# A ninth gate/up pair made inside the recurrence, and the values of segments 54 to 57 made in the opening

## The chip, the core and the metric

One core of a Trainium2 chip. The time is the device time of one execution in microseconds; the kernel before was timed three times, and its median counts. A second figure is used beside it: the span of one profiled execution, whose trace gives every row that is quoted.

## What is computed

A pre-norm block over 2048 rows of 640 columns: `h = x + A(layernorm(x))`, then `h2 = h + B(layernorm(h))`.

```
for s in range(64):                              # A: 64 segments of 32 rows
    h = concat([mem, xs])                        # 8 memory rows + 32 rows of x
    q, k, v = h Wq, h Wk, h Wv                   # 32 heads of 128
    p = softmax(where(mask, q k^T * scale, -1e9))
    o = (p v) Wo
    mem = o[:8]; outs.append(o[8:])              # the next segment's memory
# B: h = relu(x Wgate) * (x Wup), 1728 columns; out = h Wdown
```

The memory rows make A a chain: segment s+1 needs the first eight output rows of segment s. B has no such chain.

## The kernel before

Every instruction is added to a list, in program order, by hand; a solver (L46) turns the tiles that each reads and writes into semaphore waits, and each engine then runs its own instructions strictly in that order. So the place of an `add` or `dma` in the program is its place in its engine's queue. `dma` (L353) uses SP's queue where nothing else is said. A PSUM bank is a tile of its own (`B(n)`): a product that writes it waits for the copy that read it last. The banks are BQ (0, 1), T0, T1 (2, 3) and P0 to P3 (4 to 7).

**The opening** (L765 to L1134) loads the weights: Wk, Wq, Wv (`W`, 15 loads) and Wo (8 loads, L787). It makes segment 0 as soon as its weights are there, and some projections for later segments. `far_part` (L853) makes keys and queries of the late rows of segments 54 to 57 from `a3`, rows of x that depend on no memory. `far_tok` (L861) copies the banks P0 and P1 to `tok` on ScalarE, `far_flip` (L864) transposes them on VectorE, `far_save` (L868) keeps them in DRAM (`next_d[2]`, `next_d[3]`). Other held rows are saved at L1127 by `held_saves`. While the second half of Wo lands in quarters, the loop at L1120 puts one quarter of `wo_pass`, one chunk of a value projection (`xe`) and `keep_busy(2)` (L1072, matmuls whose result nobody reads) behind each other. Then come the load of the next 128 rows into `xl` (`ln1_load`, L1129), `to_act_split` (L1130, the memory rows for step 1), the copies of the banks BQ to `Ve[0]` (L1132) and the moments of `xl` (`row_moments`, L1134, on VectorE).

**The steps** (L1145 to L1339): one per segment, 1 to 63. Each projects keys (to P2, P3), the previous segment's x part, queries (to P0, P1), values, scores, softmax, and the products with Wo. `project` (L395) uses four 32-column strips of the array per chunk and half. `fill_of` (L1139) says, step by step, how many of these matmuls are split in two or load their weights again. `extra_units` (L961) puts a fourth piece into most steps: in the steps with `r = 0, 1, 2` of a group of four it projects keys, queries and values of the late rows of the next four segments. In the steps of `EARLY_STEPS` (L937) it makes a gate/up pair of B's first row block instead (`early_product`, L939): 128 of the 1728 columns, 40 matmuls of 512 columns. Its weights come through `xt` (gate) and `at` or `xl` (up) by `early_weights` (L932), its rows through the free `Ke`, `Qe`, `Ve` buffers by `early_rows` (L919); ScalarE applies relu, VectorE multiplies, and the result is kept in `hx_d`. The early steps are 50, 51, 54, 55, 56, 58, 59 and 60. Where a step is early, the projection that it would have made has been made in the opening: the keys of segments 54 to 57 (step 50), their queries (step 51), and the three of segments 58 to 61. They are loaded back in step 52 (L1167) and in step 57 (`load_next`, L1002, and L1290). Step 52 itself projects the values of segments 54 to 57.

SP's queue in a step: merges of V (`merge_v`, L694), transposes (`flip_rows`, L375), row loads, stores of attention rows.

**The feed-forward stage** (L1410 on): the pairs that were not made early are made by `gate_up` (L1026). Pairs NE to NE+3 are put between the parts of the last segment, and the others follow in the loop over blocks at L1455. `GROUPS` (L885) cuts the columns of Wg and Wu into the loads of `load_piece` (L893); the first NE pairs' columns come last, for blocks 1 to 3. `down_pair` makes the output.

## Time and profile before

| | us |
|---|---|
| median of three timed runs (979.43 to 980.81) | 980.7 |
| the profiled execution's own time | 978.38 |
| its span | 976.6 |
| PE busy in the span | 952.2 |
| VectorE (DVE) busy | 726.0 |
| ScalarE (ACT) busy | 523.0 |

How to read it: the chain of waits follows the last instruction back to what released it, so its shares say which engine sets the end. A timeline row has start, duration, engine, line, operation, output and inputs, count, and in brackets how long the engine stood idle before it and what ended that. Where a row stands for several matmuls that overlap, its duration is from the first start to the last end. SPq is SP's queue; its rows are the issue of a transfer and not the transfer itself.

### The profile page before, as it was taken

What the parts mean: (1) busy time and instruction counts of PE and PEld (TensorE: products, weight loads), DVE (VectorE), ACT (ScalarE), POOL (GpSimd) and SP (SyncE); (2) the same over time, 40 slices, a digit from 0 to 9 for tenths busy, and PEclk for the clock granted to TensorE, in tenths of its full rate; (3) what the DMA queues carried; (4) which work ended last, traced back from release to release, by engine and by line L of the source; (5) the groups of instructions that cost most, each with busy time, mean ns of one, the idle gap of its engine ahead of it and who ended that gap; (6) DMA issues with size and microseconds to landing.
All of it is one profiled execution on the core that took longest, in us unless ns stands there. A gap on an engine that the chain in (4) does not pass through costs nothing.

```text
span 976.6 us, 56721 instructions
## 1 busy us (share of the span) xinstructions
PE 952.2 (98%) x26145; PEld 535.0 (55%) x24933; DVE 726.0 (74%) x2041; ACT 523.0 (54%) x1326; POOL 186.8 (19%) x425
## 2 busy tenths in 40 slices
PE   4889999999999999999999999999999999999998
PEld 1345565655565666565556555666666665444443
DVE  3568888888888888888888888887888883545232
ACT  1466666666666666666666666655655552122120
POOL 7121112121313131313131313020201110000000
PEclk9999999999999999999999999999999999999999
DMA  9951111121222222232232323132425248603000
GB/s 359 417 213 51 46 48 42 45 52 52 55 63 54 62 55 65 56 67 57 63 60 57 62 56 61 37 103 68 102 59 139 55 139 270 208 22 94 21 14 28
DMA packets 93044, 87.35 MB, mean 89 GB/s; under 512 B 56250, under 2 KB 76546, under 8 KB 90754
## 3 DMA queue, kind: packets, MB, share of 16 engines
q1 hardware_dynamic: 91072, 82.76, 29.3%
q8 instruction: 201, 3.29, 1.4%
q10 hardware_dynamic: 1730, 0.96, 0.3%
q14 instruction: 41, 0.34, 0.1%
HBM read 46.55 MB, written 11.35 MB: 59 GB/s over the span
## 4 chain that ended last, share of the span: by engine, by line
PE 94%; SPq 3%; DMA 2%; issue 0%; POOL 0%; DVE 0%; POOLq 0%
PE ps L416 47%; PE ps L1040 9%; PE ps L614 7%; PE ps L389 7%; PE ps L631 7%; PE ps L680 4%; SPq L354 3%; PE ps L1353 3%; PE ps L915 3%; PE ps L512 2%; PE ps L709 2%; DMA Wo<-in_A_Wo_dram 2%; PE ps L566 1%; PE ps L1053 0%; PE ps L1366 0%
## 5 line engine op out<-in xcount | busy, mean ns | idle before, releaser
L416 PE MATMUL ps<-W,act_r 128*32 128x512 bf16 (+1 forms) x8357 | 463.5, 359 | 0.4 <-ACT tok L440 0.4
L416 PEld LDWEIGHTS ps<-W,act_r 128*32 128x32 bf16 x8357 | 218.5, 96 | 164.1 <-DVE act_r L660 20.7
L440 ACT ACTIVATE tok<-ps 128x512 bf16<-128x512 f32 x182 | 105.3, 594 | 59.0 <-PE ps L416 48.0
L440 ACT ACTIVATE tox<-ps 128x512 bf16<-128x512 f32 x138 | 81.8, 598 | 58.7 <-PE ps L416 48.4
L435 DVE STREAM_TRANSPOSE Ko<-tox 128x512 bf16<-128x512 bf16 x128 | 89.1, 697 | 30.3 <-ACT tox L440 29.4
L416 PE MATMUL ps<-W,act_e 128*32 128x512 bf16 x1032 | 99.0, 382 | 3.9 <-DVE TBf L493 1.5
L594 DVE STREAM_TRANSPOSE oT<-tox 128x512 bf16<-128x512 bf16 x128 | 94.9, 741 | 0.0
L435 DVE STREAM_TRANSPOSE Qo<-tok 128x512 bf16<-128x512 bf16 x124 | 85.5, 690 | 0.9
L614 PE MATMUL ps<-Wo,oT 128*32 128x160 bf16 x4032 | 81.5, 233 | 2.2 <-DMA Wo<-in_A_Wo_dram 2.2
L631 PE MATMUL ps<-Wo,oT 128*32 128x320 bf16 x2016 | 79.9, 299 | 0.5 <-DMA Wo<-in_A_Wo_dram 0.3
L614 PEld LDWEIGHTS ps<-Wo,oT 128*32 128x32 bf16 x4032 | 70.2, 97 | 12.4 <-DVE oT L588 2.8
L440 ACT ACTIVATE Vp<-ps 128x512 bf16<-128x512 f32 x127 | 75.1, 592 | 0.5 <-ACT Vp L440 0.5
L389 PE MATMUL ps<-W,act_e 128*32 128x512 bf16 x728 | 71.6, 383 | 0.0
L1068 ACT ACTIVATE g<-ps 128x512 bf16<-128x512 f32 x44 | 25.6, 594 | 78.4 <-PE ps L1040 77.0
L647 ACT ACTIVATE SA<-TA 64x40 f32<-64x40 f32 x126 | 29.6, 235 | 65.2 <-DVE TA L644 64.5
L528 ACT ACTIVATE Pm<-ps 128x64 bf16<-128x64 f32 x126 | 28.3, 224 | 66.5 <-PE ps L512 66.5
L588 DVE STREAM_TRANSPOSE oT<-om 128x128 bf16<-128x128 bf16 x126 | 39.1, 310 | 31.1 <-ACT om L580 31.1
L631 PEld LDWEIGHTS ps<-Wo,oT 128*32 128x32 bf16 x2016 | 51.0, 96 | 18.4 <-DMA Wo<-in_A_Wo_dram 1.1
L512 PE MATMUL ps<-Qo,Ko 128*32 128x40 bf16 x2048 | 61.0, 181 | 0.0
L512 PEld LDWEIGHTS ps<-Qo,Ko 128*32 128x32 bf16 x2048 | 46.5, 94 | 25.3 <-DVE Qo L435 17.9
L520 POOL COPY Qo<-ends 128x256 bf16<-128x256 bf16 x32 | 14.1, 441 | 238.1 <-DVE oT L588 220.9
L1069 DVE TENSOR_TENSOR hT<-g,ps 128x512 bf16<-128x512 bf16 x44 | 30.3, 688 | 37.8 <-PE ps L1040 33.8
(157 smaller groups left out, 1528.1 us busy)
## 6 DMA issues: line engine op xcount, KB each, us to landing
VM<-Vp SPq DMA_DIRECT2D x126, 65.0 KB
VM<-Vp SPq DMA_DIRECT2D x63, 130.0 KB
W<-in_A_Wk_dram SPq DMA_DIRECT2D x5, 1024.0 KB
W<-in_A_Wq_dram SPq DMA_DIRECT2D x5, 1024.0 KB
W<-in_A_Wv_dram SPq DMA_DIRECT2D x5, 1024.0 KB
Wo<-in_A_Wo_dram SPq DMA_DIRECT2D x8, 640.0 KB
attn_d<-wtok SPq DMA_DIRECT2D x248, 7.5 KB
xt<-in_A_x_dram SPq DMA_DIRECT2D x16, 160.0 KB
```

Source lines behind the costliest of these rows:

```text
L389: return pe.add_instruction(mybir.InstMatmult(name=nc.get_next_instruction_name(), engine=mybir.EngineType.PE, ins=[pe.lower_ap(rhs), pe.l ...
L416: ins = pe.matmul(*b, start=(c == ends[0]), stop=(c == ends[1]), skip_group_check=True)
L435: add("dve", lambda v: v.transpose(dst[:, 16 * i:16 * i + 16, 0:32], tok[t][:, :].rearrange("p (h f) -> p h f", f=32)), r=tok_keys(t), w=keys)
L440: add("act", lambda a: a.activation(dst, src, ACTF.Copy), r=r, w=w)
L512: i = pe.matmul(bank((P0, P1)[hf])[q:q + 32, o:o + 40], (Ko if a == 0 else Ke[p])[:, h, :], Qo[:, h, :], start=True, stop=True, skip_group ...
L588: add("dve", lambda v: v.transpose(ap(oT[par], 160 * hf, [[40, 4], [320, 4], [1, 8]]), ap(om, 128 * hf, [[1, 4], [4, 32]])), r=[("om", hf) ...
L594: add("dve", lambda v, kh=kh: v.transpose(ap(oT[p], 160 * kh + M, [[320, 4], [40, 4], [1, 32]]), ap(tox, 128 * kh, [[256, 4], [1, 4], [4, ...
L614: i = pe.matmul(bank(bk)[32 * gg:32 * gg + 32, 0:160], src[:, hb, 0:32], w[:, gg], start=(hb == CH[16 * halves[0]]), stop=(hb == CH[-1]), ...
L631: i = pe.matmul(bank(bk)[32 * q:32 * q + 32, 0:320], src[:, hb, 0:32], w, start=(n == 0), stop=(n == 7), skip_group_check=True)
L680: ins = pe.matmul(bank(bk)[32 * q:32 * q + 32, 0:320], src[:, hb, 0:32], w[:, 2 * (q % 2):2 * (q % 2) + 2], start=(i == 0), stop=(i == 15) ...
L1040: ins = pe.matmul(bank(bk), w[:, c, lo:lo + 128], xn2T[par][:, c, :], start=(c == 0), stop=(c == DC - 1))
L1069: add("dve", lambda v: v.tensor_tensor(hT[par][:, j, :], g1[gi][:, :], bank(bu), ALU.mult), r=[B(bu), ("g1", gi)], w=[("hT", par, j)])
```

## The change

- One pair more is made early: NE is 9, step 52 joins `EARLY_STEPS`, and `GROUPS` has one group less. Step 52 makes a pair instead of the values of segments 54 to 57.
- These values are made in the opening from `a3`: chunks (0, 1), (2, 3) and (4) behind the first three quarters of Wo, in the place of `keep_busy(2)`, into P0 and P1. ScalarE copies them to `tok[2]` and `tok[3]`, and two stores put them into `farv_d`, between the two held saves.
- Keys, queries and values of segments 54 to 57 are loaded back in step 53: the queries at its start, keys and values after its second filler. The memset of the ones beside the values moves from step 52 to step 53.
- `fill_of` has 0 instead of 26 for step 3, 28 instead of 56 for step 4, 40 instead of 56 for step 52.
- Behind the last segment two weight loads (the group that is gone) fall away, two loads of Wd move ahead of `rows`, and the loop over blocks makes one `gate_up` less in block 0.

```diff
-    NE = 8
+    NE = 9
+    farv_d = nc.dram_tensor("farv_d", [128, 8 * Dh], BF16)
...
-    GROUPS = [(EC, EC + 256), (EC + 256, EC + 512), (EC + 512, FM), (0, EC)]
+    GROUPS = [(EC, EC + 256), (EC + 256, FM), (0, EC)]
...
-              for lo, hi in (((0, 3), (3, DC)) if g == 3 else ((0, DC),))]
+              for lo, hi in (((0, 3), (3, DC)) if g == 2 else ((0, DC),))]
...
-    EARLY_STEPS = (NSEG - 14, NSEG - 13, NSEG - 10, NSEG - 9, NSEG - 8, NSEG - 6, NSEG - 5, NSEG - 4)
+    EARLY_STEPS = (NSEG - 14, NSEG - 13, NSEG - 12, NSEG - 10, NSEG - 9, NSEG - 8, NSEG - 6, NSEG - 5, NSEG - 4)
...
-    def load_next(n):
-        dma((Ke, Qe)[n][0][:].rearrange("p h t -> p (h t)"), next_d[n][:, :], r=[("next", n)],
-            w=[(("Ke", "Qe")[n], 0, i) for i in range(2)])
+    def load_next(q, n):
+        dst = ends[:, 1024 * n:1024 * n + 1024] if q else (Ke, Qe)[n][0][:].rearrange("p h t -> p (h t)")
+        dma(dst, next_d[2 * q + n][:, :], r=[("next", 2 * q + n)] + [("next", 3, i) for i in range(2) if q * n],
+            w=[(("Ke", "Qe")[n], q, i) for i in range(2)])
...
     for g in range(3):
         wo_pass(0, P3, (1,), (g,))
         project(xe, xke, 2, (0, 1), BQ, (2 + g,))
-        if g < 2:
-            keep_busy(2)
+        project(a3, k3, 2, (0, 1), (P0, P1), ((0, 1), (2, 3), (4,))[g])
+    for i in range(2):
+        to_tok((P0, P1)[i], 2 + i, "act")
     wo_pass(0, P3, (1,), (3,))
     keep_busy(3)
     for n, t, ks in held_saves:
         dma(next_d[n][:, :], ...)
+        if n == 0:
+            for i in range(2):
+                dma(farv_d[:, 512 * i:512 * i + 512], tok[2 + i], r=tok_keys(2 + i), w=[("farv", i)])
     ln1_load(1, xl, ("xl",))
...
-        n = {1: 0, 2: 0, 3: 26, 56: 40, 50: 0, ...
+        n = {1: 0, 2: 0, 3: 0, 4: 28, 52: 40, 56: 40, 50: 0, ...
...
-            if s in (NSEG - 14, NSEG - 13, NSEG - 10, NSEG - 9, NSEG - 8, NSEG - 5, NSEG - 4):
+            if s in (NSEG - 14, NSEG - 13, NSEG - 12, NSEG - 10, NSEG - 9, NSEG - 8, NSEG - 5, NSEG - 4):
                 early_weights(s, 1)
-            elif s == NSEG - 12:
-                for n in range(2):
-                    dma(ends[:, 1024 * n:1024 * n + 1024], next_d[2 + n][:, :],
-                        r=[("next", 2 + n)] + [("next", 3, i) for i in range(2) if n],
-                        w=[(("Ke", "Qe")[n], 1, i) for i in range(2)])
+            elif s == NSEG - 11:
+                load_next(1, 1)
                 add("pool", lambda p: p.memset(ap(Ve[1], Dh, [[VW, 8], [1, VW - Dh]]), 1.0),
                     w=[("Ve1", 1), ("Ve", 1, 0), ("Ve", 1, 1)])
             elif s == NSEG - 7:
-                load_next(1)
+                load_next(0, 1)
...
                 early_weights(s + 1, 1)
-                load_next(0)
+                load_next(0, 0)
                 dma(ap(Ve[0], 0, [[1, 8 * VW]]), nextv_d[:, :], ...)
-        elif s in (NSEG - 14, NSEG - 10, NSEG - 9, NSEG - 6, NSEG - 5):
+            elif s == NSEG - 11:
+                load_next(1, 0)
+                dma(ap(Ve[1], 0, [[VW, 8], [1, Dh]]), farv_d[:, :].rearrange("p (k d) -> p k d", d=Dh),
+                    r=[("farv", i) for i in range(2)] + [("Ve1", 1)], w=[("Ve", 1, 0), ("Ve", 1, 1)])
+        elif s in (NSEG - 14, NSEG - 13, NSEG - 10, NSEG - 9, NSEG - 6, NSEG - 5):
             early_weights(s + 1, 0)
...
-    for _ in range(2):
-        load_piece(("Wdone", 0))
+    for n in range(2):
+        load_down(n)
     rows(P3, s % 2, s - 1)
     gate_up(0, NE + 1)
-    for n in range(2):
-        load_down(n)
```

2 lines of the change are left out of this document (1 added, 1 removed).

## The prediction, made before the changed kernel was run

> **What bounds the kernel now.** I read the page's chain first, then the waits of PE while the opening runs, then the timelines of single engines around the three places that the diff touches: the opening (50 to 66 us), steps 52 to 54 (670 to 706 us) and the start of the feed-forward stage (820 to 840 us).
>
> ```profile
> PE 94%; SPq 3%; DMA 2%; issue 0%; POOL 0%; DVE 0%; POOLq 0%
> ```
> ```profile
> PE ps L614 <- DMA Wo<-in_A_Wo_dram: 2.2, 3, 1.2
> ```
> From 58 us on the chain is PE alone, so a microsecond of PE work taken out after that is a microsecond gained, and a microsecond in which PE is made to wait is one lost. Ahead of 58 us the end is set by the load of the weights. PE waits 2.2 us in all for quarters of Wo: there lies the idle time into which the new projection is put.
>
> ```profile
> 52.31 0.46 PE L614 MATMUL ps<-Wo,oT 128*32 128x160 bf16 x16 [1.22 <-DMA Wo<-in_A_Wo_dram]
> 52.58 0.40 PE L416 MATMUL ps<-W,act_e 128*32 128x512 bf16 x4
> 52.80 0.40 PE L389 MATMUL ps<-W,act_e 128*32 128x512 bf16 x4
> ...
> 57.08 0.46 PE L614 MATMUL ps<-Wo,oT 128*32 128x160 bf16 x16 [0.66 <-DMA Wo<-in_A_Wo_dram]
> ```
> The columns are start, duration, engine, line. A quarter of Wo occupies PE for 0.27 us (52.31 to 52.58), a set of four 32-column matmuls of 512 columns for 0.22 us (52.58 to 52.80). The last quarter lands at 57.08.
>
> **The tail: what is removed.** With nine pairs made early, the feed-forward's first block has one gate/up pair fewer behind the last segment.
>
> ```profile
> 820.84 0.16 issue
> 821.00 2.10 PE ps L1040 x9
> 823.10 1.09 PE ps L1053 x10
> ...
> 839.78 5.34 PE ps L1040 x24
> ```
> The pair is the 2.10 us between the last row sums and the tails; its ten matmuls are back to back on the chain. Gain: 2.10 us. The other four late pairs stay in their four slots. Step 52 exchanges 40 matmuls of 512 columns for 40, so PE's columns there are unchanged; its fill of 40 instead of 56, and the lower fills of steps 3 and 4, only splits fewer matmuls, and I cost it at nothing: the columns stay, and the chain, which runs through steps of all these fills, has "issue 0%". I allow 0.1 us each way for it.
>
> The gain is kept only if what comes next is there 2.1 us sooner. The second block's weights are loaded meanwhile, now 1152 columns instead of 1024, so 0.33 MB more.
>
> ```profile
> GB/s 154 237 37 221 43 156 239 100 200 106 148 390 451 419 350 392 371 347 96 75 339 355 337 358 406 405 395 387 346 365 168 49 9 189 226 269 278 274 76 130
> ```
> The slices are 1.25 us from 800 us. Transfers run from 825 to 838.7 at some 370 GB/s, the last 0.65 MB being rows that are needed later; so Wu is there by about 837.0, and with 0.33 MB more (0.9 us) by 837.9. Block 1 starts at 839.78; its first Wu product follows 1.1 us later (half a pair), and in the changed kernel 2.1 us sooner than that, at 838.8. It fits by some 0.9 us, an estimate from these slices; what they are too early by is the cost, and I bound it by 0.8 us.
>
> **The opening: what is added.** Forty matmuls (ten sets, 10 x 0.22 = 2.2 us) take the place of two short keep-busy calls. Two things make them late, and then make others late.
>
> First their banks. They write P0 and P1, which the far query rows still occupy until ScalarE has copied them out:
>
> ```profile
> 53.58 1.08 ACT L440 ACTIVATE tox<-ps 128x512 bf16<-128x512 f32 x2
> 57.77 1.08 ACT L440 ACTIVATE Ve<-ps 128x512 bf16<-128x512 f32 x2 [3.11 <-DMA next_d<-Ve]
> ```
> The second copy ends at 54.66. PE arrives at 53.02 and waits to about 54.72; behind it on PE stand the second quarter of Wo and all after it. From there: 0.86 + 0.27 (Wo) + 0.43 + 0.86 + 0.27 + 0.43 + 0.43 us, so the last value matmul is issued by 58.27 and the last quarter of Wo ends at 58.54 instead of 57.35. That is 1.2 us late for the first memory rows, even though the weights are long there.
>
> Second, and larger, SP's queue. The two stores of the new values stand in it directly after the first held store, and ahead of the load of x rows into xl:
>
> ```profile
> 41.92 0.32 SPq L354 DMA_DIRECT2D next_d<-oTe  x1
> 42.29 2.77 SPq L354 DMA_DIRECT2D xl<-in_A_x_dram  x1
> ```
> Before, that load was issued at 42.29 and lay behind Wo in the DMA queue. Now SP stands still until ScalarE has copied both banks: last matmul ends at 58.45 (its 0.40 us less the 0.22 of its pace), two copies take 1.08 us, 59.53. Then the second store, the next held store and xl are issued 0.37 us apart (41.92 to 42.29): xl at about 60.3. How long such a load takes in a quiet queue is shown by step 5, which loads as many rows into xl:
>
> ```profile
> 112.51 0.39 SPq L354 DMA_DIRECT2D xl<-in_A_x_dram  x1
> ```
> ```profile
> 114.25:114.50 0.25, 0.25 (x18) 0.17 (x8) 0.25 (x3) 0.25 (x3) 0.00 (x0) 1.00 0.27 72
> 114.50:114.75 0.25, 0.25 (x24) 0.15 (x13) 0.18 (x1) 0.25 (x2) 0.00 (x0) 1.00 0.05 10
> ```
> The last column is GB/s: the data end by 114.5, 2.0 us after the issue. With some 0.15 us for the stores ahead of it, xl lands at 62.45.
>
> [...]
>
> VectorE works in order, and the moments of xl stand ahead of step 1's key flips:
>
> ```profile
> 58.74 0.89 DVE L358 BATCH_NORM_STATS2 st<-xl 128x6 f32<-128x320 bf16 x2 [0.20 <-DMA xl<-in_A_x_dram]
> 59.66 0.21 DVE L360 BATCH_NORM_AGGREGATE mv<-st 128x2 f32<-128x12 f32 x1
> 60.17 0.71 DVE L435 STREAM_TRANSPOSE Ko<-tox 128x512 bf16<-128x512 bf16 x1 [0.30 <-ACT tox L440]
> 61.25 0.71 DVE L435 STREAM_TRANSPOSE Ko<-tox 128x512 bf16<-128x512 bf16 x1 [0.37 <-ACT tox L440]
> ...
> 62.79 0.71 DVE L435 STREAM_TRANSPOSE Qo<-tok 128x512 bf16<-128x512 bf16 x1
> ...
> 64.35 0.67 DVE L435 STREAM_TRANSPOSE Qo<-tok 128x512 bf16<-128x512 bf16 x1
> ```
> ```profile
> 65.16 0.19 PE L512 MATMUL ps<-Qo,Ko 128*32 128x40 bf16 x4
> ```
> VectorE already waits 0.20 us for xl in the kernel before. Its moments move from 58.74 to 62.45, by 3.7 us. The gaps of 0.30 and 0.37 us ahead of the two key flips take up 0.65; from 61.25 on there is no gap, so the last query flip ends 3.05 us later (65.02 to 68.07). The scores that need it are at 65.16, 0.14 us behind it: PE loses 2.9 us. PE's own lateness of 1.2 us lies inside this and isn't added. After step 1 PE is the only bound again, so the 2.9 us stay in the span.
>
> Ends of this price: if the banks were free in time, the last value would be copied by about 57.9, xl would land at 60.85, and PE would lose 1.3 us. If the load took the 2.4 us of the weight tile below, and the 0.4 MB of stores ahead of it ran first at 370 GB/s (1.0 us), it would land at 63.7 and PE would lose 4.2. I take 2.9, from the row of the same load.
>
> **Steps 52 to 54.** Step 52 gains a VectorE product, like those of step 51 today, and has one ScalarE evacuation instead of two; with "DVE 0%" in the chain nothing is charged. In step 53 SP gets four more issues: the ninth product's store and the query rows at its start, the key rows and the values after its second filler.
>
> ```profile
> 682.10 2.06 SPq L377 DMA_TRANSPOSE at<-xl  x1
> 686.24 0.53 SPq L354 DMA_DIRECT2D xl<-in_A_x_dram  x1
> ...
> 696.47 0.45 SPq L354 DMA_DIRECT2D at<-in_B_W_up_dram  x1
> ```
> ```profile
> 685.99 0.22 ACT L528 ACTIVATE Pm<-ps 128x64 bf16<-128x64 f32 x1 [0.49 <-PE ps L512]
> ```
> ```profile
> L915 PE MATMUL ps<-Ke,at x8: 379/379/379, 700.5 to 702.9; 128*32 128x512 bf16 x8
> ```
> The xl load here follows the first exponential (ends 686.21), not the transpose, so the first two issues, about 0.9 us, are at least partly hidden. The last two, 0.45 us each like the row of 696.47, push W_up's tile for step 54 to 697.4, or 698.3 with nothing hidden. What such a load takes:
>
> ```profile
> 706.61 0.42 SPq L354 DMA_DIRECT2D at<-in_B_W_up_dram  x1
> ```
> ```profile
> 708.75:709.00 0.25, 0.25 (x12) 0.11 (x8) 0.25 (x2) 0.25 (x1) 0.00 (x0) 1.00 0.41 85
> ```
> 2.4 us: it lands at 699.8 to 700.7, and PE wants it at 700.5. I take nothing; the upper end is 0.5 us, if one of SP's longer issues falls here. The values' load lands before the next step's value products for the same reason.
>
> **Sum.** -2.10 (tail) + 2.9 (opening) + 0 (step 53) = +0.8 us on the profiled execution, 978.38 us (span 976.6). That run lies 2.3 us below the median of the three timed runs; the difference is added to the median: 980.7 + 0.8 = **981.5 us**. A difference of 0.2% is 2.0 us, about what a measurement of this kernel can tell from no change.
>
> **Rivals.**
> - The new stall replaces the gain in half: the banks come free in time, or xl lands sooner. Opening 1.3, sum -0.8, 979.9 us. For it: the lower end above. Against: the copies that end at 54.66 are in order on ScalarE behind work that nothing moves.
> - The opening is free, as idle time of 2.2 us for 2.2 us of work would suggest. Sum -2.1, 978.6 us. Against it speaks the row in which VectorE waits for xl already.
> - Slower, by PE's pace. PE is idle from 51.1 to 52.3 and would be again from 53.0 to 54.7, with the keep-busy calls gone. That PE runs slowly after idling is seen at the start:
>
> ```profile
> 17.92 0.65 PE L389 MATMUL ps<-W,act_e 128*32 128x512 bf16 x4
> 18.35 0.51 PE L416 MATMUL ps<-W,act_e 128*32 128x512 bf16 x4
> 18.69 0.39 PE L389 MATMUL ps<-W,act_e 128*32 128x512 bf16 x4
> ```
>   A set lasts 0.65 us until 18.35 and 0.39 after it, at pitches of 0.43 and 0.22. If PE fell to that pace at 54.7, the 3.5 us of work to 58.3 would take some 1.7 us more for half of it, all of it ahead of xl: sum +2.5, 983.2 us. [...]
> - The tail gives less than 2.1 us because Wu is late: up to 0.8 us, sum +1.6, 982.3 us.
>
> **How the numbers follow.** Forecast 0.60 (0.03 of it over +0.2%, where xl lands as late as the upper end), half-priced opening 0.14, free opening 0.08, slow pace 0.12, late Wu 0.06 (0.01 over +0.2%). Faster by over 0.2% is the free opening alone: 0.08. Slower by over 0.2%: 0.03 + 0.12 + 0.01 = 0.16. Within 0.2%: 0.76. The range goes from 979.3 (half-priced opening, with 0.6 us of the runs' own spread) to 983.4 (slow pace); the free opening and a sum of two costs are left out.
>
> **What would show it.** Tail: the tails directly after the last row sums, block 1 starting 16.8 us after those instead of 18.9, no wait for Wu. Opening: a PE wait of 1.7 us for ScalarE at 53 us; the moments of xl at 62.4 with VectorE waiting over 2 us for the load; step 1's second scores at 68.1 instead of 65.16, and every step after it as late. Steps 53 and 54: no PE wait for a DMA. The prediction is wrong if the moments of xl start before 61, if the matmuls of 53 to 58 us last 0.65, or if PE waits in step 54.

## The result, and the profile after

| | us |
|---|---|
| kernel before, median in the runs that measured both | 979.58 (978.61 to 980.81) |
| changed kernel, median | 985.31 (984.79 for the five runs of 983.85 to 988.39 alone) |
| ratio, 95% interval | 1.0058 [1.0038, 1.0078] |

The change costs 0.58%, some 5.7 us; 981.5 was forecast. A sixth execution of the changed kernel took 2002 us, with PE busy for 1979 us instead of some 957; the ratio leaves it out, and so does the profile after, which is that of the same kernel's next run (e1 below), 988.06 us with a span of 986.3. Its lines are numbered one (from the feed-forward stage on two or more) higher than those of the kernel before.

The page's chain, and the waits of PE (total, times, longest), of the changed kernel:

```profile
PE 90%; DMA 5%; SPq 2%; DVE 1%; ACT 1%; issue 1%; POOL 0%; DVEq 0%; POOLq 0%
```
```profile
PE ps L417 <- ACT tox L441: 2.1, 1, 2.1
...
PE ps L513 <- DVE Qo L436: 1.6, 1, 1.6
PE ps L710 <- DMA VM<-Vp: 1.5, 1, 1.5
PE ps L681 <- issue: 1.5, 1, 1.5
...
PE ps L567 <- DVE Pbd L535: 1.0, 1, 1.0
PE ps L615 <- DMA Wo<-in_A_Wo_dram: 1.0, 1, 1.0
PE ps L1042 <- ACT g L1070: 0.9, 1, 0.9
```

PE's share of the chain falls from 94 to 90%. One old wait (for Wo) is shorter; six new ones stand beside it, and each belongs to a place: the opening (L417, L513), step 54 (L710), step 58 and the last row sums (L567, L681), the second feed-forward block (L1042).

Where they act is read from one event that comes once a step: the start of the x products (`pv_x`, L709 before, L710 after). This table gives how late it is against the kernel before, from the timelines of PE; "to the end" is the span less the start of the last of these products (976.6 - 811.64 = 165.0 before).

| late by, us | step 1 | step 2 | 53 | 54 | 55 | last | to the end |
|---|---|---|---|---|---|---|---|
| before: starts at | 60.50 | 72.42 | 681.93 | 693.94 | 706.03 | 811.64 | 165.0 |
| changed (e1) | 3.08 | 5.06 | 5.59 | 7.25 | 7.45 | 9.77 | 164.9 |
| e2 opening alone | 1.67 | 3.79 | 4.07 | 4.05 | 4.00 | 5.23 | 165.7 |
| e3 without the opening | 0.10 | 0.10 | 0.27 | 2.29 | 4.18 | 4.40 | 165.0 |
| e4 stores behind xl | 3.05 | 3.69 | 4.27 | 6.13 | 7.93 | 8.96 | 166.1 |
| e5 step 53 reordered | 2.95 | 4.92 | 5.91 | 5.97 | 7.94 | 9.60 | 164.7 |
| e6 free banks | 0.08 | 1.25 | 1.95 | 3.39 | 4.44 | 4.62 | 164.0 |
| e7 both | -0.47 | 0.43 | 2.09 | 2.78 | 3.12 | 3.64 | 164.0 |
| e8 gap filled | 2.54 | 3.84 | 4.17 | 4.17 | 4.37 | 5.25 | 166.8 |
| e9 order by need | -0.57 | 0.64 | 1.95 | 1.96 | 5.34 | 5.36 | 164.2 |
| e10 weights earlier | 0.21 | 1.47 | 2.33 | 2.74 | 3.26 | 4.07 | 162.5 |
| e12 loads left out | -0.58 | 0.55 | 1.78 | 1.78 | 1.67 | 2.50 | 163.8 |
| e15 before, weights earlier | 0.14 | 0.15 | 0.66 | 1.01 | 0.90 | 1.61 | 164.9 |

Each row is one execution. e15 has nothing of the change ahead of the last segment and is 1.6 us late there: the profiled execution of before (978.38 us, 1.2 under the median above) is a quick one, and a row of the last column but one carries that much of chance. What happens at one place, with a wait that names it, is firm; a sum over sixty steps is not.

For the changed kernel the columns add up: opening 5.06, steps 2 to 53 0.53, steps 53 and 54 1.86, the steps from 55 on 2.32, tail -0.1; 9.7 us, which is the 988.06 - 978.38 = 9.68 between the two profiled executions. The medians differ by less, 5.7 here and 6.0 in e1: the profiled execution is the slowest of e1's six. Of the 2.32 us one wait of 1.0 has a name: in step 58 PE waits for VectorE, which waits for the landing of a store of attention rows. No other profile has such a wait there, so it can't be put down to the change.

**The opening after.** Timeline of PE in the changed kernel:

```profile
52.43 0.40 PE L390 MATMUL ps<-W,act_e 128*32 128x512 bf16 x4
54.91 0.40 PE L417 MATMUL ps<-W,act_r 128*32 128x512 bf16 x4 [2.08 <-ACT tox L441]
...
55.35 0.65 PE L417 MATMUL ps<-W,act_r 128*32 128x512 bf16 x4
...
58.02 0.65 PE L390 MATMUL ps<-W,act_r 128*32 128x512 bf16 x4
...
58.81 0.39 PE L390 MATMUL ps<-W,act_r 128*32 128x512 bf16 x4
...
60.17 0.45 PE L615 MATMUL ps<-Wo,oT 128*32 128x160 bf16 x16
```

PE waits for the banks (forecast 1.7, measured 2.1), then its sets last 0.65 instead of 0.39 us until 58.4, and the last quarter of Wo is at 60.17 instead of 57.08. Behind that come xl's issue and VectorE's moments:

```profile
62.35 0.45 SPq L355 DMA_DIRECT2D xl<-in_A_x_dram  x1
```
```profile
64.92 0.89 DVE L359 BATCH_NORM_STATS2 st<-xl 128x6 f32<-128x320 bf16 x2 [3.30 <-DMA xl<-in_A_x_dram]
```

The queue held xl back as forecast, from the slower start: 62.35 instead of 60.3, moments at 64.92 instead of 62.45.

### The profile page after: what moved, and what is told of

The parts are those of the page before. It is cut to its first block, busy times and chain, and to the rows that moved or that the text cites. A ratio compares the mean times of both kernels' runs of the same rounds, so it can differ in the third digit from the quotient of the medians.

```text
span 2000.6 us, 56707 instructions
## 1 busy us (share of the span) xinstructions
PE 1979.2 (99%) x26144; PEld 882.9 (44%) x24916; DVE 745.5 (37%) x2041; ACT 527.7 (26%) x1326; POOL 185.4 (9%) x425
## 3 DMA queue, kind: packets, MB, share of 16 engines
q8 instruction: 201, 3.29, 0.7%
## 4 chain that ended last, share of the span: by engine, by line
PE 99%; DMA 1%; issue 0%; ACT 0%; POOL 0%; DVE 0%; ACTq 0%; POOLq 0%
PE ps L417 50%; PE ps L1042 9%; PE ps L390 9%; PE ps L632 7%; PE ps L615 7%; PE ps L681 4%; PE ps L1360 3%; PE ps L916 3%; PE ps L513 2%; PE ps L710 2%; PE ps L567 1%; DMA wtok<-in_A_mem_dram 1%; PE ps L1055 0%; PE ps L1373 0%; ACT tox L441 0%
## 5 line engine op out<-in xcount | busy, mean ns | idle before, releaser
L417 PE MATMUL ps<-W,act_r 128*32 128x512 bf16 (+1 forms) x8336 | 949.3, 627 | 1.2 <-ACT tox L441 1.2
L417 PEld LDWEIGHTS ps<-W,act_r 128*32 128x32 bf16 x8336 | 339.3, 141 | 454.3 <-issue 362.4
L417 PE MATMUL ps<-W,act_e 128*32 128x512 bf16 x1008 | 175.4, 675 | 1.7 <-DVE TBf L494 1.7
L632 PE MATMUL ps<-Wo,oT 128*32 128x320 bf16 x2016 | 163.1, 506 | 0.0
L615 PEld LDWEIGHTS ps<-Wo,oT 128*32 128x32 bf16 x4032 | 142.0, 147 | 26.8 <-issue 3.3
L390 PE MATMUL ps<-W,act_e 128*32 128x512 bf16 x712 | 125.1, 682 | 0.0
L632 PEld LDWEIGHTS ps<-Wo,oT 128*32 128x32 bf16 x2016 | 85.6, 149 | 63.8 <-issue 16.0
L1360 PE MATMUL ps<-Wd,hT 128*128 128x320 bf16 (+4 forms) x225 | 106.1, 498 | 0.0
L1042 PE MATMUL ps<-xn2T,Wu 128*128 128x512 bf16 x195 | 99.5, 678 | 0.0
L390 PE MATMUL ps<-Wd,hT 128*128 128x320 bf16 x195 | 97.8, 502 | 0.0
L1042 PE MATMUL ps<-xn2T,Wg 128*128 128x512 bf16 x186 | 95.5, 680 | 2.3 <-issue 2.3
L513 PE MATMUL ps<-Qo,Ko 128*32 128x40 bf16 x2048 | 90.3, 231 | 0.0
L513 PEld LDWEIGHTS ps<-Qo,Ko 128*32 128x32 bf16 x2048 | 69.9, 120 | 38.3 <-issue 38.0
L681 PE MATMUL ps<-Wo,oTe 128*32 128x320 bf16 x1024 | 85.0, 505 | 0.0
```

Source lines behind the costliest of these rows:

```text
L390: return pe.add_instruction(mybir.InstMatmult(name=nc.get_next_instruction_name(), engine=mybir.EngineType.PE, ins=[pe.lower_ap(rhs), pe.l ...
L417: ins = pe.matmul(*b, start=(c == ends[0]), stop=(c == ends[1]), skip_group_check=True)
L513: i = pe.matmul(bank((P0, P1)[hf])[q:q + 32, o:o + 40], (Ko if a == 0 else Ke[p])[:, h, :], Qo[:, h, :], start=True, stop=True, skip_group ...
L615: i = pe.matmul(bank(bk)[32 * gg:32 * gg + 32, 0:160], src[:, hb, 0:32], w[:, gg], start=(hb == CH[16 * halves[0]]), stop=(hb == CH[-1]), ...
L632: i = pe.matmul(bank(bk)[32 * q:32 * q + 32, 0:320], src[:, hb, 0:32], w, start=(n == 0), stop=(n == 7), skip_group_check=True)
L681: ins = pe.matmul(bank(bk)[32 * q:32 * q + 32, 0:320], src[:, hb, 0:32], w[:, 2 * (q % 2):2 * (q % 2) + 2], start=(i == 0), stop=(i == 15) ...
```

## Experiments

All were timed in five rounds beside the kernel before on the same chip. Ratios are to that kernel. In the first four, theory A is SP's queue in the opening, B PE's pace there, C steps 52 to 54 or the tail. The letters have new meanings in each later group, given in the expectations; D is the added bytes of step 53, T the loads of the tail, Q the queue of step 1.

| run | median us | before | ratio [95%] |
|---|---|---|---|
| e1 changed kernel again | 986.17 | 980.21 | 1.0054 [1.0039, 1.0069] |
| e2 opening alone | 986.09 | 980.21 | 1.0058 [1.0046, 1.0070] |
| e3 without the opening | 981.39 | 980.21 | 1.0009 [0.9998, 1.0021] |
| e4 stores behind xl | 985.86 | 980.21 | 1.0056 [1.0037, 1.0074] |
| e5 queue of step 53 | 984.70 | 980.32 | 1.0057 [1.0039, 1.0074] |
| e6 free banks | 982.49 | 980.32 | 1.0034 [1.0021, 1.0047] |
| e7 banks and queue | 981.41 | 980.32 | 1.0012 [1.0002, 1.0021] |
| e8 gap filled | 985.46 | 980.32 | 1.0055 [1.0043, 1.0067] |
| e9 order by need | 982.97 | 979.59 | 1.0035 [1.0022, 1.0049] |
| e10 weights earlier | 979.99 | 979.59 | 1.0009 [1.0000, 1.0018] |
| e11 need and weights | 982.05 | 979.59 | 1.0025 [1.0013, 1.0037] |
| e12 loads left out | 981.05 | 979.59 | 1.0014 [1.0005, 1.0023] |
| e13 stores behind saves | 981.10 | 980.02 | 1.0010 [0.9995, 1.0025] |
| e14 and xl behind merges | 981.80 | 980.02 | 1.0019 [1.0009, 1.0029] |
| e15 before, weights earlier | 979.89 | 980.02 | 1.0003 [0.9994, 1.0011] |
| e17 no loads, all edits | 981.25 | 980.38 | 1.0015 [1.0000, 1.0029] |
| e18 weights earlier, again | 982.42 | 980.38 | 1.0015 [1.0004, 1.0026] |

### e1 to e4: which part costs it

e1 is the changed kernel. e2 is the kernel before with the opening's edits alone (and the fills of steps 3 and 4, not shown):

```diff
-        if g < 2:
-            keep_busy(2)
+        project(a3, k3, 2, (0, 1), (P0, P1), ((0, 1), (2, 3), (4,))[g])
+    for i in range(2):
+        to_tok((P0, P1)[i], 2 + i, "act")
...
+            for i in range(2):
+                dma(farv_d[:, 512 * i:512 * i + 512], tok[2 + i], r=tok_keys(2 + i), w=[("farv", i)])
```

e3 is the changed kernel without these (the values of segments 54 to 57 are replaced by other data of the same size), e4 the changed kernel with the two stores moved:

```diff
+    ln1_load(1, xl, ("xl",))
     for i in range(2):
         dma(farv_d[:, 512 * i:512 * i + 512], tok[2 + i], r=tok_keys(2 + i), w=[("farv", i)])
-    ln1_load(1, xl, ("xl",))
```

> The changed kernel as it is, for a profile in which PE runs at full pace. Theory A (SP's queue): VectorE waits for xl until about 62.4 us, step 1's second scores at about 68.1 instead of 65.16, tail 2.1 us shorter; that accounts for +0.8 us only, so the rest of the measured 5.7 us must show at another place. Theory B (PE's pace): the mean granted clock is below 1.00, and a stretch of half-pace matmuls (0.65 us a set instead of 0.39) lies in or behind the opening; two thousandths of clock over 980 us are 4 us at half pace, so 2 us lost. Theory C (steps 52 to 54 or the tail): PE waits for a DMA there, or block 1's start waits, for 2 us or more.

> The kernel before with only the opening's part of the change: the values projected between Wo's quarters, copied and stored (and the fills of steps 3 and 4); nobody loads them, and step 52 projects its values as before. The output is complete. Theory A alone: +2.9 us against the kernel before. Theory A with B: +5 to +8 us, all that the change lost and the 2.1 us of the tail besides. Theory C: at most +3 us.

> The changed kernel without the opening's part: the keep-busy calls are back, and the store into the values' place takes rows of the kept queries instead, so that the values of segments 54 to 57 are wrong data; all loads, the ninth pair and the tail are there. Theories A and B: 2.1 us faster than the kernel before, mean clock 1.00. Theory C: no faster, or slower.

> The changed kernel with the two stores of the values behind the second held store and the load of xl in SP's queue. Theory A: xl lands as early as before, what is left of the opening's price is PE's lateness of 1.2 us, so 1.7 us less than the changed kernel, whatever else it loses. Theory B: the gap in front of the value matmuls stays, so the low clock stays; the time falls by at most 1.7 us. Theory C: unchanged within 1 us.

The opening alone costs as much as the whole change (986.09 against 986.17), and without it 4.8 of the 6.0 us are gone. In e2's profiled execution PE waits as long as in e1, 2.24 us, but keeps its pace:

```profile
55.18 0.40 PE L417 MATMUL ps<-W,act_r 128*32 128x512 bf16 x4 [2.24 <-ACT tox L441]
...
58.76 0.45 PE L615 MATMUL ps<-Wo,oT 128*32 128x160 bf16 x16
```

The granted clock (third column from the right) of the stretch from 55 to 59 us, in e1 and then in e2:

```profile
55.00:59.00 4.00, 4.00 (x56) 1.30 (x39) 0.70 (x2) 0.00 (x0) 0.12 (x1) 0.57 0.23 88
```
```profile
55.00:59.00 4.00, 3.82 (x104) 1.72 (x76) 0.97 (x2) 0.15 (x2) 0.12 (x1) 1.00 0.24 93
```

So the pace is the clock's: 0.57 against 1.00 behind much the same wait, 60.17 against 58.76 for the last quarter, 1.4 us. This execution of e2 is the opening without the slow clock, 3.79 us late at step 2; e1 is the one with it, 5.06. In e4, with the slow clock and xl ahead of the stores, only 0.64 us are added between steps 1 and 2, where e1 adds 1.98 and e2 2.12: the stores ahead of xl cost some 1.4 us. Theories A and B hold both. The median of e4 doesn't fall, though, as theory A said it would: steps 53 and 54 cost 3.7 us in its profiled execution, 1.8 more than in e1, with a second stretch of slow clock.

Every timed run has a mean granted clock, and it parts the times. Of the eleven runs of the changed kernel (without the one of 2002 us) nine have 0.998 and average 986.3 us; the two at 1.000 took 982.72 and 983.93. In e4 the three runs at 1.000 took 981.9 to 983.2 us, the five at 0.996 to 0.998 took 985.5 to 989.2. In e2 only the profiled run has 1.000, and it is the fastest of five. Of the 19 runs of the kernel before beside them none is under 0.999. So the low clock came in most runs of the kernels with this wait (e1, e2, e4), and some 3 us of the 6 come with it; an estimate from few runs, and more than the 1.4 us that the trace of the opening shows.

e3 has another loss, which was not forecast. SP's queue in step 53 of e3, and PE:

```profile
684.69 1.23 SPq L378 DMA_TRANSPOSE at<-xl  x1
689.78 0.54 SPq L355 DMA_DIRECT2D xl<-in_A_x_dram  x1
...
691.76 2.54 SPq L355 DMA_DIRECT2D VM<-Vp  x3
```
```profile
696.23 0.72 PE L710 MATMUL ps<-VM,Px 64*32 64x129 bf16 x32 [1.86 <-DMA VM<-Vp]
696.89 2.22 PE L417 MATMUL ps<-W,act_r 128*32 128x512 bf16 x20
```

Before, the transpose was issued at 682.10, the load into xl at 686.24 and the merges VM<-Vp at 688.73. Now two issues stand ahead of the transpose; the load into xl waits for the landing of the transpose, which reads xl, and the merges, which PE needs for `pv_x`, stand behind that load, 3.0 us later than before. PE waits 1.86 us, and behind the wait 20 matmuls take 2.22 us (1.26 in e5, 700.26). Steps 53 and 54 cost 2.0 and 1.9 us here, 1.9 together in e1, 3.7 in e4.

### e5 to e8: undoing each cause

e5 moves two issues in step 53:

```diff
             elif s == NSEG - 11:
-                load_next(1, 1)
...
                 flip_rows(chunks_of(at[:, :]), xl, ("xl",), ("at",))
-                if more:
+                if s == NSEG - 11:
+                    load_next(1, 1)
+                elif more:
                     ln1_load(nb + 1, xl, ("xl",))
...
         merge_v(s, 0)
+        if s == NSEG - 11 and more:
+            ln1_load(nb + 1, xl, ("xl",))
```

e6 takes other banks, and stores behind xl as e4 does; e7 is e5 and e6 together:

```diff
-        project(a3, k3, 2, (0, 1), (P0, P1), ((0, 1), (2, 3), (4,))[g])
-    for i in range(2):
-        to_tok((P0, P1)[i], 2 + i, "act")
+        if g < 2:
+            project(a3, k3, 2, (g,), ((T1, T0)[g],))
+            to_tok((T1, T0)[g], 2 + g, "act")
```

e8 is e4 with the wait filled:

```diff
+        if g == 0:
+            keep_busy(9)
         project(a3, k3, 2, (0, 1), (P0, P1), ((0, 1), (2, 3), (4,))[g])
```

> The changed kernel with two issues of step 53 moved in SP's queue: the query rows' load behind the transpose of xl instead of ahead of it, the next load into xl behind the three merges of Vp into VM instead of ahead of them. The same loads, the same bytes. Theory A (order of SP's queue: the merges are issued 1 to 2.8 us late because the load into xl stands ahead of them and waits for the transpose): the merges are issued less than 0.6 us later than in the kernel before, counted from the start of the step, PE's wait for VM in step 54 (1.5 to 1.9 us) is gone, and with it the slow pace behind it; steps 53 to 54 and 54 to 55 last 12.0 and 12.1 us again instead of 13.6 to 14.0 and 12.4 to 14.0. Time 1.9 to 3.9 us under the changed kernel's 986: 982 to 984. Theory D (the added transfers themselves, 0.5 MB of keys, query rows and values, take the bandwidth from the merges): order changes nothing, PE still waits over 1 us for VM, 985 to 987.

> The changed kernel with the new values projected into the banks T1 and T0, which nobody occupies at that time, one half in each of the first two places, each copied out right behind its projection, and the two stores of the values behind the load into xl. Theory A (PE's gap of 2.2 us for the banks, the slow pace that follows it in some executions, and xl's load behind the stores are all that the opening costs): no PE wait for ScalarE at 53 us, all sets 0.39 to 0.40 us, the last quarter of Wo within 0.4 us of the kernel before (57.1 to 57.7), step 2 within 0.5 us of it. Time 3.7 to 5.1 us under the changed kernel: 981 to 982.5. Theory B (40 matmuls more cost their own 2.2 us wherever they stand): step 2 still about 2 us late, 983 to 984.

> Both edits together: values in free banks with their stores behind xl, and step 53's issues reordered. By theory A in both places all that is left is the tail's 2.1 us: 977.7 to 978.9 beside 980.2 of the kernel before, faster by 0.13 to 0.25 per cent. By theory D in step 53: 980 to 982. By theory B in the opening: 980 to 981. If the tail gives less than 2.1 us because the second block's weights come late, block 1 waits for Wu and the time stays at 979 to 980.5.

> The kernel with the stores behind the load into xl and the banks P0 and P1 (step 2 was 3.7 us late in it, PE's sets lasted 0.65 us from 55.8 to 58.9), with nine keep-busy matmuls of 512 columns (9 x 0.22 = 2.0 us) ahead of the first set of the new values, in the 2.2 us in which PE waits for the banks. Clock theory (idling for some 2 us drops PE to half pace for 3 to 3.5 us): the sets of 54.7 to 59 us last 0.39, the last quarter of Wo ends near 58.9 instead of 60.4, step 2 is some 2 us late instead of 3.7; time some 1.5 us less, about 984.3. Rival (the slow pace comes from the copies or the transfers that run beside it): 0.65 stays, time about 986.

e6: no wait for the banks, no slow pace, and the forty matmuls fit into the time of the two keep-busy calls and of the waits for Wo. The last quarter is where it was before the change (57.08):

```profile
52.67 1.26 PE L417 MATMUL ps<-W,act_r 128*32 128x512 bf16 x20
...
54.46 1.26 PE L417 MATMUL ps<-W,act_r 128*32 128x512 bf16 x20
...
57.16 0.46 PE L615 MATMUL ps<-Wo,oT 128*32 128x160 bf16 x16 [0.66 <-DMA Wo<-in_A_Wo_dram]
```

That settles theory B of these runs (forty matmuls cost their 2.2 us wherever they stand): up to step 1 they cost nothing, it is 0.08 us late. e4 and e6 both have the stores behind xl and differ in the banks, with the matmuls divided to fit them: at step 2 they are 3.69 and 1.25 us late, and their ratios are 1.0056 and 1.0034. The median falls by 2.8 to 3.7 us against the changed kernel's 985.3 to 986.2. 1.25 us stay at step 2; e13 looks at that.

e5: step 53 is mended (12.07 us) and step 54 lasts 14.06, and half of the 2.0 us too much is a wait for W_up's tile, which is late now:

```profile
708.42 0.40 PE L916 MATMUL ps<-Ke,at 128*32 128x512 bf16 x4 [0.96 <-DMA at<-in_B_W_up_dram]
```

The wait moved one transfer on, and the time hardly changed: its order of the queue is not a cure. In e7 the merges are issued 6.1 us after the step's x products, sooner than the 6.8 of the kernel before, and PE waits for no transfer in steps 53 and 54; they still cost 1.0 us, 0.42 of it a stop of PE without a releaser. So the order of the queue made PE wait for the merges, as theory A says; whether the rest is theory D's 0.75 MB more in ten microseconds isn't shown by these runs.

e8: the clock theory's sign is there, no set is longer than 0.40 us, and the granted clock is 1.00 where e4 has 0.59; nothing else that the matmuls ran beside was taken away. By itself that is a sign and no proof, as e2's profile has 1.00 behind the wait. Its size isn't there: the quarter of Wo ahead of it came 1.5 us later than in e4 (53.17 instead of 51.71), step 2 is 3.84 us late, and the three runs of e8 at a clock of 1.000 took 985.2 to 985.9 us. Filling the wait cost what it saved.

### e9 to e12: bytes in step 53, loads in the tail

e9 is e7 with W_gate's tile and the rows behind the merges too, and W_up's tile ahead of the row stores:

```diff
-            if s in (NSEG - 14, NSEG - 13, NSEG - 12, NSEG - 10, NSEG - 9, NSEG - 8, NSEG - 5, NSEG - 4):
+            if s in (NSEG - 14, NSEG - 13, NSEG - 12, NSEG - 9, NSEG - 8, NSEG - 5, NSEG - 4):
                 early_weights(s, 1)
...
-            if s in (NSEG - 15, NSEG - 11, NSEG - 7):
+            if s in (NSEG - 15, NSEG - 7):
                 early_weights(s + 1, 0)
...
         merge_v(s, 0)
-        if s == NSEG - 11 and more:
+        if s == NSEG - 11:
+            early_weights(s + 1, 0)
+            early_rows(1 - place(s + 1)[0], 2, 4)
             ln1_load(nb + 1, xl, ("xl",))
...
             ln1_back(nb, chunks_of(at[:, :]), [("at",)], "pool")
+            if s == NSEG - 11:
+                early_weights(s + 1, 1)
```

e10 is e7 with the second block's loads issued earlier:

```diff
     load_down(4)
+    dma(xn2T[1][:, :, :], xn2_d[:, :, TB:2 * TB], r=[("Wdone", 2)] + [("xn2_d", u) for u in range(4, 8)],
+        w=[("xn2", 1, u) for u in range(4)])
+    load_rows(0, [("Wdone", 1)])
+    while pieces:
+        load_piece(("hT", 0, NE + 2))
     rows(P2, (s + 1) % 2, s)
     woe_pass(P3, range(16))
     woe_sum(P3)
     woe_store(NSEG // 4 - 1)
```

(the same calls are taken away behind `woe_store` and in the loop over blocks). e11 is both. e12 is e7 without the three loads, so segments 54 to 57 compute with other data:

```diff
-                    load_next(1, 1)
...
-                load_next(1, 0)
-                dma(ap(Ve[1], 0, [[VW, 8], [1, Dh]]), farv_d[:, :].rearrange("p (k d) -> p k d", d=Dh),
-                    r=[("farv", i) for i in range(2)] + [("Ve1", 1)], w=[("Ve", 1, 0), ("Ve", 1, 1)])
```

> The kernel with free banks and step 53's two moved issues, and three more issues of step 53 put in the order in which they are needed: the merges of Vp ahead of W_gate's tile and of the rows, W_up's tile for step 54 behind the keys and values and ahead of the stores of the rows instead of behind them. The same bytes. Theory A (order of SP's queue): the merges land some 2 us sooner, W_up's tile is issued 3 us sooner; PE waits neither for VM nor for W_up in step 54, steps 53 to 54 and 54 to 55 last 12.0 and 12.1 us; time some 1 us under the 981.4 of the kernel it starts from: 980.2 to 980.8. Theory D (too many bytes in 10 us): PE waits for something else there (rows, keys), the steps stay 0.7 to 2 us longer, 981 to 982.

> The kernel with free banks and step 53's two moved issues, and the loads for the feed-forward's second block (xn2T, the h rows, the last pieces of Wg and Wu, 4.1 MB) issued ahead of the last rows' stores, into the 6 us in which the transfers rest, instead of behind them. Theory T (the removed pair's 2.1 us are half given back because the second block's weights now hold up the output store, with it the osb buffer, VectorE, the load of the attention rows and ScalarE, for which PE waits 0.5 to 1.3 us at the ninth product of block 1): the first output store lands sooner, PE waits for no ScalarE in block 1; from the last pv_x to the end 163.2 to 163.6 us instead of 164.0; time 980.5 to 981. Theory F (PE's stalls without a cause in the profile, 0.6 to 2.2 us in the last row sums, come some 2.5 us after a 16 KB instruction packet that loads of weights hold up): the stall stays or grows, 981 to 982.

> Both edits together: by theories A and T steps 53 and 54 cost nothing, the tail gives 1.5 to 2.1 us, the opening costs about 0.5: 979.0 to 980.0 beside 980.3 of the kernel before. If D or F holds: 980.5 to 982.

> The kernel with free banks and step 53's two moved issues, without the loads of the keys, the query rows and the values of segments 54 to 57 in step 53: those segments compute with whatever the buffers hold, so the output is another one; the ninth product of step 52, its store and all of PE's work stay. Theory D (the three loads, 0.75 MB, and their issues cost what steps 53 and 54 cost): no PE wait for VM or W_up, steps 53 to 54 and 54 to 55 last 12.0 and 12.1, time some 1 us under 981.4. If the ninth product itself (its store, its slot) costs it: 981.4.

Step 53: without the three loads, steps 53 and 54 last 12.01 and 11.98 us. With them and the better order of e9, step 53 lasts 12.02, but xl, now behind W_gate and the rows, is 3 us late for VectorE, and PE waits for VectorE:

```profile
698.21 0.88 DVE L359 BATCH_NORM_STATS2 st<-xl 64x6 f32<-64x320 bf16 x2 [2.98 <-DMA xl<-in_A_x_dram]
```
```profile
701.98 0.20 PE L513 MATMUL ps<-Qo,Ko 128*32 128x40 bf16 x4 [2.52 <-DVE Qo L436]
```

e11 repeats it (2.50 us). So in these profiles each order made another transfer late (the merges, W_up's tile, xl), and e12, without the loads, has none late. That speaks for theory D, but the time doesn't: D gave e12 some 1 us less than e7, and the two stand at 1.0014 and 1.0012. e17 below goes against it too. D is not shown.

The tail: in e7 only 0.9 of the removed pair's 2.10 us are gained (164.96 to 164.0). VectorE, SP and PE in e7:

```profile
844.21 0.89 DVE L1384 TENSOR_TENSOR osb<-ps,h 128x320 bf16<-128x320 f32 x2 [1.42 <-DMA out_dram<-osb]
848.37 0.49 DVE L742 TENSOR_TENSOR h<-xt,at 128x640 bf16<-128x640 bf16 x1 [1.36 <-DMA at<-attn_d]
```
```profile
829.20 1.15 SPq L355 DMA_DIRECT2D Wg<-in_B_W_gate_dram  x2
...
835.27 10.19 SPq L355 DMA_DIRECT2D out_dram<-osb  x4
845.50 0.43 SPq L355 DMA_DIRECT2D xt<-in_A_x_dram  x1
845.98 0.46 SPq L355 DMA_DIRECT2D at<-attn_d  x1
```
```profile
851.13 1.25 PE L1042 MATMUL ps<-xn2T,Wg 128*128 128x512 bf16 x5 [0.53 <-ACT g L1070]
```

Block 1 starts at 841.79, only 12.6 us after its weights are issued (15.1 before, 824.64 to 839.78). The first output store is issued behind these weights, its buffer is not free for the fourth output tile (VectorE waits 1.42 us for it), SP's queue stands at the four stores (10.19 us; before 8.75, from 833.03), the attention rows for the next block are loaded 4.2 us into block 1 instead of 2.5, and ScalarE, which must do their layer norm first, frees PE's bank late. PE waits 0.5 to 1.3 us for it in e1, e3, e4, e5, e6, e7, e9 and e12. In e10 the loads are issued ahead of the last rows' stores; there is no such wait, and the tail is 162.5, 2.5 us under before. Theory T holds: with the loads of before, the pair's gain is lost again behind them. e15 shows that the earlier loads gain nothing by themselves: without the pair's removal the tail is 164.9 and the ratio 1.0003.

### e13 to e18: what is left

e13 is e10 with the two stores behind the four saves of step 1; e14 is e11 with this and with xl's load directly behind the merges:

```diff
                 far_save(1)
+                for i in range(2):
+                    dma(farv_d[:, 512 * i:512 * i + 512], tok[2 + i], r=tok_keys(2 + i), w=[("farv", i)])
```
```diff
+            ln1_load(nb + 1, xl, ("xl",))
             early_weights(s + 1, 0)
             early_rows(1 - place(s + 1)[0], 2, 4)
-            ln1_load(nb + 1, xl, ("xl",))
```

e15 is the kernel before with e10's tail edit alone, e17 is e13 without the three loads (other data again in segments 54 to 57), e18 is e10 once more.

> The kernel with free banks, step 53's two moved issues and the earlier weights, with the two stores of the new values behind the four saves of step 1 (ends, far queries and keys) instead of ahead of them. In the kernel it starts from, steps 1 to 2 last 12.8 to 13.2 us instead of 11.9: the stores wait until 55.7 us for ScalarE's copies, the saves behind them are issued at 58 to 61 us instead of 46 to 56, the transpose of xl (issued at 64.7 as before) lands after 4.4 us instead of 2.8, the load into xl waits for it, and with it the merges of step 1. Theory Q (this queue is all that is left of the opening's cost): the transpose lands within 3 us, steps 1 to 2 last 12.0 us, step 2 is at most 0.4 us late; 979.0 to 979.4 where the kernel before takes 979.6 to 980.3. Rival (the 40 matmuls or the bytes stored cost it): steps 1 to 2 still 12.8 us or more, 980.

> The same, and in step 53 the load into xl directly behind the merges, then W_gate's tile and the rows, and W_up's tile ahead of the stores of the rows. In the kernel in which xl stood behind W_gate's tile and the rows, VectorE waited 3.0 us for xl's moments and PE 2.5 us behind it; in the one without W_up moved, steps 53 and 54 cost 0.5 to 1.0 us. Theory A (order): no wait of PE in steps 53 and 54, 12.0 and 12.1 us; 978.4 to 978.9. Theory D (bytes): 0.5 us or more stay, 979 to 980.

> The kernel before the change with the tail's edit alone: xn2T, the h rows and the last pieces of Wg and Wu issued ahead of the last rows' stores. Theory T (it is the removed pair that brings block 1 too close behind the loads): here PE waits for nothing in block 1, so the edit changes nothing, 979.6 to 980.3. If the edit gains 0.5 us or more here too, what it gave the changed kernel is not the pair's 2.1 us come back.

> The kernel with free banks, the stores of the new values behind step 1's saves, the merges of step 53 ahead of xl's load and the earlier weights, without the loads of the keys, the query rows and the values of segments 54 to 57 (those segments compute with whatever the buffers hold, so the output is another one). It closes the account: by theories Q, D and T the opening costs 0 to 0.4 us, or 1.4 where xl's transpose lands late, steps 53 and 54 nothing, and the tail gives 2.1 to 2.5 us: 977.6 to 979.0 beside some 980 of the kernel before, the first of these kernels that is faster than that. If the ninth product, its slot or the stores cost something that is not accounted for: 979.5 or more.

> The kernel with free banks, step 53's two moved issues and the earlier weights once more, for the fastest of the kernels that compute the reference's output: 980.0 against 979.6 at first. By the accounts so far (opening 0.4 to 1.5, steps 53 and 54 0.5 to 1, tail -2.5, and the chance stalls of steps 42 to 62) it stays within 0.2 per cent of the kernel before: ratio 0.999 to 1.002. If the tail's gain were larger than the rest in most executions it would be under 0.999.

e15: nothing, as theory T says. e13 and e14 have the same opening, and in one the steps 1 to 2 last 13.10 us, in the other 12.34 (before 11.92; e10 13.18, e18 13.39). The difference is the transpose of xl again; e13, then e14:

```profile
64.77 1.33 SPq L378 DMA_TRANSPOSE at<-xl  x1
69.12 0.34 SPq L355 DMA_DIRECT2D xl<-in_A_x_dram  x1
```
```profile
64.11 1.32 SPq L378 DMA_TRANSPOSE at<-xl  x1
66.86 0.35 SPq L355 DMA_DIRECT2D xl<-in_A_x_dram  x1
```

Its packets are through by 67.2 and by 66.5, and SP goes on 1.9 us after that in e13, 0.4 in e14. So theory Q falls: the saves' place in the queue doesn't decide it, and what does stays open. In e14 all of the opening's cost is gone at step 2 (0.01 us late). Its order of step 53, with xl directly behind the merges, is no cure either: steps 53 and 54 cost 3.1 us, and this time VectorE waits 2.8 us for a store of attention rows and PE 1.46 us for VectorE.

e17 should have closed the account and doesn't: 981.25, not 979. In its profiled execution (985.02) PE stands 2.38 us in the last row sums and 0.90 and 0.66 us at other places, with nothing that the profile names as releaser; steps 53 and 54 take 0.7 and 1.1 us more although their loads are gone, and in step 54 xl is late again:

```profile
697.11 0.88 DVE L359 BATCH_NORM_STATS2 st<-xl 64x6 f32<-64x320 bf16 x2 [1.75 <-DMA xl<-in_A_x_dram]
```

So the same code of step 53 has this wait in e17 and not in e12, both without the loads, and theory D does not account for it. e18 repeats e10's code at 1.0015. No version here that makes the ninth pair beats the kernel before; e10 and e13 come nearest, within 0.1 to 0.15% of it. One loss of theirs has no name: in every kernel with free banks (e6, e7, e9 to e14, e17, e18) the stretch from step 2 to step 53 adds 0.7 to 2.2 us to the lateness, in the others 0.2 to 1.0. No wait of 0.45 us or more stands there, and why is open.

## Why the prediction was wrong

Three steps failed: that PE would keep its pace, that steps 52 to 54 cost nothing, and that the tail keeps its gain. In e1's profile they are 1.3, 1.9 and 2.0 of the 8.9 us between +0.8 and +9.7; 0.9 are the opening's two waits, and 2.8 come in steps 2 to 53 and from 55 on, of which 1.0 has a name. Two of the three signs of being wrong that the prediction gave came: sets of 0.65 us, and a wait of PE in step 54.

**Opening, +2.9 forecast: right in both mechanisms, too small.** PE's wait for ScalarE's copies was 2.1 to 2.4 us instead of 1.7, and xl's load behind the stores set step 1, as forecast. Without the slow clock the part measures 3.8 (e2), inside the forecast ends of 1.3 and 4.2; with it 5.1, outside.

**PE's pace: the first failed step.** The rival "slower, by PE's pace" got a chance of 0.12. It came in three of the four profiled openings with this wait (e1, e4, e5; not e2), and nine of the eleven runs of the changed kernel have the low mean clock. One row of the trace of before speaks against it, a gap of 1.22 us that was followed by full pace (0.40 us a set). The gap forecast was 1.7 us, above every gap that the trace of before could vouch for. The length of the wait alone doesn't part the cases: the slow clock came behind 1.78 us in e4 and not behind 2.24 us in e2.

**Steps 52 to 54, 0 forecast: the second failed step.** "At least partly hidden" was said of two issues ahead of the transpose, with the argument that the load into xl follows the first exponential and not the transpose. It waits for both. SP's waits in step 53, before and in e3:

```profile
SPq L124 <- DMA at<-xl: 1.2, 1, 1.2
```
```profile
SPq L124 <- DMA at<-xl: 3.8, 1, 3.8
```

Before, the issue of the transpose ended at 684.16 and the wait for its landing at some 685.4, 0.8 us ahead of the exponential: all the cover there was. And what it covered was not the load into xl alone but the merges behind it. The upper end of 0.5 us should have counted who waits for the queue: 1.9 us in e1, 3.9 in e3. e5 and e7 show the merges' part; about 1 us of steps 53 and 54 stays open.

**Tail, -2.10 forecast: the third failed step.** The pair went, the tails follow the last row sums as forecast, and Wu was in time, as the working said; but the tail is 0.1 us shorter in e1 and 0.8 to 1.0 in e6, e7 and e9. The prediction asked of the time between the weights' issue and block 1 only whether Wu lands. What it left out: the same shortening held up the output stores behind the weights, and the attention rows behind the stores, so PE waits 0.5 to 1.3 us for ScalarE. e10 shows it, with the loads earlier and the gain kept. In e1 a stall of 1.48 us in the last row sums takes the rest; it is of the kind described below, and e2, with the tail of before, has one of 0.78.

**The sum.** Forecast 2.9 - 2.1 + 0 = +0.8. Measured in the runs of the change's parts: the opening 4.8 (e1 less e3), the rest 1.2 (e3 less before) instead of -2.1. The opening alone is 5.9 (e2 less before), so the parts and the whole agree to some 1 us only, and e17 didn't close the account. The forecast's base, 980.7, lay 1.1 us above the 979.58 of the later runs; that brought the number nearer to the measured one by luck.

## What to carry to other kernels

A moved issue was paid in SP's queue here by what stands behind the next wait (the merges of step 53, issued 3.0 us later in e3), so follow the queue from the moved issue to the first transfer that the bounding engine needs, and compare with the slack of that one. Before giving new matmuls to a waiting PE, look for banks that nobody holds: here the same forty matmuls cost some 2 to 3 us more in occupied banks than in free ones (e4 against e6). A gap longer than any that the trace shows to be harmless is a risk to be priced: here nine of the eleven runs of the changed kernel had the low mean clock. When work ahead of a fixed batch of loads is removed, ask what else travels behind these loads, not only whether they land in time.

## What the runs showed of the hardware

**The clock fell behind seven waits of ten.** Of ten waits of PE of 1.78 to 2.52 us in these traces (behind 50 us), seven were followed by a stretch of low granted clock (e1, e4 and e5 in the opening, e3 and e4 in step 54, e11 there, e8 in the tail), three were not (2.24 us in e2, 2.52 in e9, 2.38 in e17). None of the shorter ones, up to 1.57 us in e1, was. In e1's stretch the clock is 0.50:

```profile
55.40:58.70 3.30, 3.30 (x48) 1.08 (x28) 0.30 (x1) 0.00 (x0) 0.12 (x1) 0.50 0.19 71
```

The tail of e8, where PE stood for 2.19 us until 828.47:

```profile
828.40:832.00 3.60, 3.53 (x25) 1.98 (x25) 0.48 (x1) 0.43 (x2) 0.00 (x0) 0.53 0.02 5
```

**17 of 22 PE stalls without a releaser ended 2.3 to 2.8 us after the start of an instruction packet.** The transfers of a quarter microsecond of e1 (packets, MB, share), and the stall in its chain:

```profile
q1 hardware_dynamic: 75, 0.09, 101.1%
q8 instruction: 1, 0.02, 28.4%
```
```profile
826.26 4.08 PE ps L681 x120
830.34 1.48 issue
831.81 0.48 PE ps L681 x8
```

The packet is in the stretch from 829.25, PE goes on at 831.81. The profiles of e1 to e18 have 22 such stalls of 0.45 us or more behind 50 us, the longest of 2.38 us. In 17 of them a packet of the instruction queue started 2.3 to 2.8 us before PE went on; in five (e3, e4, e13 and two in e14) none did. The page has 201 such packets in a span, one in 5 us, so a chance meeting would be the exception. That a late packet is the cause was not tested; most of these packets run beside many others, as the loads of weights and rows bring them, but one of e8 runs alone. On the page the 201 packets are 3.29 MB, some 16 KB each; what makes PE stand is open. The profiled execution of before has no such stall of 0.45 us, that of e17 has three that add up to 3.9 us.

**A load that waits for a transpose by DMA stood up to 2.5 us past the transpose's last packet**: 1.9 us in e13's step 1 (above), 2.5 in e3's step 53 (the packets are through by 687.3 and the load behind it is issued at 689.78). In e14's step 1 it is 0.4 us. Why stays open.
